# The first segment's P @ V runs: a fourth block only when more than ten blocks wait

## The chip, the cores and the metric

The kernel runs on one core of a Trainium2 chip. The metric is the device time of one launch in microseconds (us). Several launches are timed, and one more is taken with the hardware profiler; traces and profile pages come from that one.

## The reference

The input is one sequence of 2048 tokens with 512 features, all fp32. Two attention branches with 32 heads of 16 dimensions read the same `x`, and a gate per token mixes them:

```python
x = A_x
g = _sigmoid((x * gate_w).sum(-1, keepdims=True))
a = _A_ref(x, A_wqkv, A_wo)
b = _B_ref(x, B_wq, B_wk, B_wv, B_wo, B_beta)
return g * a + (1 - g) * b
```

`_A_ref` is plain softmax attention over all 2048 keys, with an output projection. `_B_ref` cuts the sequence into four segments of 512. In each it takes causal softmax attention within the segment, adds a read of a linear memory built from the earlier segments (`num / den`, mixed by `sigmoid(beta)`), and projects the result with its own `wo`.

## The kernel before

**Stages.** The first stage, up to about 345 us, computes Q, K and V of both branches (`pr`, line 312) and the memory terms, and writes them to DRAM. The second stage is the attention, and the change lies there. At the end come the output projections (`piece`, line 748), most of them laid between the attention's instructions.

**Units and slots.** The attention is cut into units. A unit is a side (A or B), a group of four heads (`g`, 8 of them) and a segment of 512 queries (`c`, 4 of them). A unit of A takes 64 slots, a unit of B takes 10. The order is A, B, A, B, and so on, so that a pair takes 74 slots; the first segment (`c` = 0) covers slots 0 to 591, since `first["A", 0, 1]`, the first slot of the second segment, is 8 x 74 = 592. In all there are 2368 slots.

**What a slot does.** The program is written out slot by slot, each engine in that order, by the loop at the end of `gated_mix`:

- `score_part(n)` puts one 128 x 512 tile of transposed scores into PSUM (matmul `st`, line 615, three buffers) and lets ScalarE take its exponential into `p` (line 638; 635 for some of B). Four slots fill one tile of `p`, of which there are six: four key-by-query blocks with four heads each. With a tile's last slot its four blocks go into `queue`, each with the slot from which it may be used (3 slots later for A, 5 for B). On side B, GpSimd first masks the diagonal (line 619).
- `max_part(n + 96)` runs 96 slots ahead. It puts scores in the other orientation into one of four PSUM banks (matmul `sm`, line 205), and VectorE reduces them to row maxima (line 220 for A; lines 235, 241 and 245 for B, where ScalarE and GpSimd prepare half of the tiles, lines 231 and 232). Every slot before the last 96 has one such tile.
- Once a unit's maxima are complete, they are merged (lines 181 to 189), transposed (`mt_ps`, line 195) and written into rows of `q`, so that the score matmul subtracts them itself.

The score matmuls contract over 48 or 50 rows at partitions 0 or 64; `st` and `sm` of one slot mostly lie in different halves of the array.

**Bursts and runs.** After every third slot comes a burst: `some_values` takes blocks from the head of `queue` and multiplies them with V (matmul `ops`, line 671, one PSUM bank). Blocks that are neighbours in one tile of `p` make one run of up to 512 columns, with one matmul for each of the four heads, at four column positions of the array; a run can't cross from one tile of `p` to the next. These are full fp32 matmuls, and the trace shows two records for each, so that one run of four heads reads "x8". A burst takes up to three blocks, and a fourth where more than six wait:

```python
some_values(n, MOST + (len(queue) > 6) if n < nS else 8)
```

A burst ends with the last block of a unit; ScalarE then copies the result out (line 675). The blocks that arrive (one per slot on average) and the three that a burst takes balance over three slots. `queue` counts all that wait, also those that may not be used yet. In the second and third segments other work takes the place of some bursts (`shared`), or is added to them (`fill`); in the first segment neither has an entry.

Of the kernel before, what the change touches and what calls it, by code (L numbers as in the profile page):

```python
# [37 lines left out]
MOST = 3  # L38
# [10 lines left out]
def gated_mix(ctx, tc, x, xT, wqkv, a_wo, b_wq, b_wk, b_wv, b_wo, beta, gate_w, out):  # L49
# [52 lines left out]
    first = {}  # L102
# [5 lines left out]
    nS = len(slots)  # L108
# [143 lines left out]
    def run_todo(m):  # L252

        for e in [e for e in todo if e[0] <= m]:
            todo.remove(e)
            e[1]()

    def run_late(pool, tag, m):
        for e in [e for e in late if e[0] < m]:
            late.remove(e)  # L260
            transpose_max(e[1], e[2], pool, tag)
# [3 lines left out]
    def loads(m):  # L265

        m = min(m, len(maxs) - 1)
        while loaded[0] <= m:
            u, (r, i) = maxs[loaded[0]]
            if loaded[0] == first_max[u]:  # L270
                load_q(u)
            kc = u[2] if u[0] == "B" else i // 8
            if (u, kc) not in kt_:
                load_k(u, kc)
            loaded[0] += 1
# [322 lines left out]
    queue = []  # L598
# [51 lines left out]
    def some_values(n, most):  # L650

        while queue and most and queue[0][0] <= n:
            _, u, i = queue.pop(0)
            most -= 1
            side, g, c = u
            w = 1
            while (queue and most and queue[0][0] <= n and queue[0][1] == u and (i + w) // 4 == i // 4
                   and (side == "A" or PIECES[i + w][0] == PIECES[i][0])):
                queue.pop(0)
                most -= 1  # L660
                w += 1
            p = pt_[u, i // 4]
            if side == "A":
                c0 = q0 = 128 * (i % 4)
                v = vt[u][:, i // 16, i // 4 % 4]
            else:
                b, c0, q0 = PIECES[i]
                v = vt[u][:, b]
            done = i + w == SLOTS[side]
            for h in range(4):  # L670
                nc.tensor.matmul(ops[32 * h:32 * h + 17, q0:q0 + 128 * w], v[:, 17 * h:17 * h + 17], p[:, h, c0:c0 + 128 * w],  # L671
                                 start=(i == 0), stop=done, tile_position=(0, 32 * h))
            if done:
                raw = ob.tile([128, CH], F32, tag="o", name="oraw")
                nc.scalar.copy(raw, ops)
                nc.sync.dma_start(od[side, c][4 * g:4 * g + 4].rearrange("h r t -> (h r) t"), raw)
                stored.add(u)
                if side == "B" and c and g % 2 == 0:
                    octet("M", g // 2, c, n + 4)
                if (side, g ^ 1, c) in stored and u != ("A", NG - 1, NCH - 1):  # L680
                    octet(side, g // 2, c, n + 8)
                if side == "A" and c - 1 in SHARED:
                    shared.extend(half_block(c - 1, g // 2, g % 2))
                return
# [89 lines left out]
    def half_block(c, b, half):  # L774

        ps = ops[:, 0:256]
        ks = [(side, o) for o in range(NO) for side in "AB"]
        for i in range(16):
            def f(i=i):
                piece(ps, *ks[i // 2], c, b, 2 * half + i % 2, i == 0, i == 15)  # L780
                if i == 15:
                    t = fr.tile([128, D], F32, tag="res", name="res", bufs=2)
                    nc.scalar.copy(t[:, 0:256], ps)
                    nc.sync.dma_start(out_rows(c, b)[:, 256 * half:256 * half + 256], t[:, 0:256])
            yield f
# [32 lines left out]
    def close(n, side, o, b, j):  # L818
        def f():
            if (side, o) == closing[0] and j == 0:  # L820
                assert len(free) == 4
            piece(banks[b], side, o, last, b, j, (side, o) == closing[0] and j == 0, (side, o) == closing[-1] and j == 3)
        fill.append((n, f))
    for side, o in closing[:-1]:
        for b in range(4):
            for j in range(4):
                close(max(tail0, end[side, 2 * o + 1, last] + 56), side, o, b, j)

    filled = [0]
    n = 0  # L830
    while n < nS or queue or beside or filled[0] < len(fill):
        for f in beside.pop(n, []):
            f()
        if n < nS:
            score_part(n)
        m = n + LEAD
        if m < nS:
            loads(m + PRE)

            def bank():  # L840
                i = free.pop(0)
                free.append(i)
                return banks[i]
            max_part(m, bank)
        run_todo(m)
        if n % BURST == BURST - 1 or n >= nS:
            if shared:
                for _ in range(4):
                    shared.pop(0)()
            else:  # L850
                some_values(n, MOST + (len(queue) > 6) if n < nS else 8)

            if any(e[0] < m + 1 for e in late):
                run_late(st_ps, "st", m + 1)
            else:
                for _ in range(1 if m < nS else 2):
                    if filled[0] < len(fill) and fill[filled[0]][0] <= n:
                        fill[filled[0]][1]()
                        filled[0] += 1
        n += 1  # L860
# [11 lines left out]
def build():  # L872
    import concourse.bacc as bacc
    nc = bacc.Bacc("TRN2", target_bir_lowering=False, num_devices=1)
    shapes = {"x": (S, D), "xT": (D, S), "wqkv": (D, 3 * D), "a_wo": (D, D), "b_wq": (D, D), "b_wk": (D, D),
              "b_wv": (D, D), "b_wo": (D, D), "beta": (H,), "gate_w": (D,)}
    args = [nc.dram_tensor(n, s, F32, kind="ExternalInput").ap() for n, s in shapes.items()]
    out = nc.dram_tensor("out", (S, D), F32, kind="ExternalOutput").ap()
    with tile.TileContext(nc) as tc:
        gated_mix(tc, *args, out)  # L880
    return nc
# [23 lines left out]
```

## Time and profile before

| | |
|---|---|
| three timed launches | 1939.02, 1941.87, 1943.77 us; median 1941.87 us |
| the profiled launch | 1940.47 us, its span 1938.8 us |
| mean granted TensorE clock | 0.993 |
| busy by engine | PE 98%, VectorE (DVE) 83%, ScalarE (ACT) 76%, GpSimd (POOL) 15% |

The span is the time from the program's first to its last instruction on the core; 1.67 us of the launch lie outside. The busy share of PE counts matmuls whose ends are modelled, and up to several of them overlap, so that it says less than that of VectorE and ScalarE. PEld is the weight load of a matmul, which may run beside an earlier matmul. In lists of instructions in order of time, neighbours of one kind are merged: "1.05 ... x8" is one run of eight records that took 1.05 us from the first start to the last (modelled) end.

### The profile page before, as it was taken

The numbers are of one execution on the slowest core, as the hardware profiler recorded it, in microseconds if no ns is written. First come the engines' busy times: TensorE is split into PE (matmuls) and PEld (weight loads), VectorE is DVE, ScalarE is ACT, GpSimd is POOL, SyncE is SP. The second block draws the span as 40 slices with busy tenths as digits, with TensorE's granted clock in tenths as the row PEclk, the third lists the DMA queues.
The fourth block names the chain that finished last, engine by engine and source line by source line (L and its number), as shares of the span: only waits on it lengthen the run. The fifth ranks groups of instructions, "written<-read, shape, count | busy, mean of one in ns | idle before, by whom it ended". The sixth has DMA issues, their size and how long they took to land.

```text
span 1938.8 us, 44063 instructions
## 1 busy us (share of the span) xinstructions
PE 1897.4 (98%) x17009; PEld 993.5 (51%) x17009; DVE 1611.9 (83%) x2768; ACT 1467.0 (76%) x2859; POOL 281.7 (15%) x497
## 2 busy tenths in 40 slices
PE   7999999999999999999999999999999999999997
PEld 6888766444444444444444444444444455555545
DVE  4235687899999999999999999999999889889810
ACT  3234432788888888888888888888888787878874
POOL 3000000211111111121111111111111111111210
PEclk9999999899999999999999999999999999999999
DMA  6667645434233334343444344434334333333211
GB/s 204 204 228 254 201 155 166 114 101 133 85 107 84 107 85 119 91 117 91 118 93 116 103 105 104 104 105 107 105 104 105 101 93 102 101 105 96 80 53 40
DMA packets 123632, 227.16 MB, mean 117 GB/s; under 512 B 35064, under 2 KB 48920, under 8 KB 122912
## 3 DMA queue, kind: packets, MB, share of 16 engines
q1 hardware_dynamic: 121840, 223.24, 41.0%
q8 instruction: 135, 2.21, 0.5%
q0 software_dynamic: 1296, 0.59, 0.2%
q14 instruction: 73, 0.60, 0.1%
q10 hardware_dynamic: 288, 0.52, 0.1%
HBM read 155.52 MB, written 67.52 MB: 115 GB/s over the span
## 4 chain that ended last, share of the span: by engine, by line
PE 89%; DMA 3%; ACT 3%; DVE 3%; issue 1%; POOL 0%; SPq 0%; ACTq 0%; POOLq 0%; DVEq 0%
PE ops L671 30%; PE st L615 27%; PE sm L205 14%; PE pr L312 11%; PE ops L748 3%; PE sm L748 2%; ACT p L638 2%; DVE pm L220 1%; DMA qdA<-q 1%; PE num L469 1%; DMA kdB<-q 1%; PE mt_ps L195 1%; ACT dg L231 1%; PE mps L500 0%; DMA qdB<-q 0%
## 5 line engine op out<-in xcount | busy, mean ns | idle before, releaser
L638 ACT ACTIVATE p<-st 128x512 f32<-128x512 f32 x2304 | 1219.5, 605 | 205.8 <-PE sm L205 168.7
L220 DVE TENSOR_REDUCE pm<-sm 128x1 f32<-128x512 f32 x2048 | 1286.5, 682 | 94.1 <-PE sm L205 71.3
L205 PE MATMUL sm<-kA,qA 48*128 48x512 f32 x2048 | 757.7, 450 | 1.3 <-DVE pm L220 1.3
L615 PE MATMUL st<-qA,kA 50*128 50x512 f32 x2048 | 702.9, 439 | 7.8 <-ACT p L638 7.1
L671 PE MATMUL ops<-p,vA 128*17 128x512 f32 (+2 forms) x4912 | 561.2, 529 | 0.0
L615 PEld LDWEIGHTS st<-qA,kA 50*128 50x128 f32 x2048 | 336.1, 186 | 412.6 <-ACT p L638 336.9
L205 PEld LDWEIGHTS sm<-kA,qA 48*128 48x128 f32 x2048 | 338.3, 185 | 37.7 <-DVE pm L220 22.9
L205 PE MATMUL sm<-kB,qB 48*128 48x128 f32 (+2 forms) x896 | 171.5, 295 | 0.6 <-DVE pmB L241 0.5
L671 PEld LDWEIGHTS ops<-p,vA 128*17 128x17 f32 x4912 | 81.7, 95 | 165.0 <-issue 153.9
L205 PEld LDWEIGHTS sm<-kB,qB 48*128 48x128 f32 x896 | 135.0, 188 | 10.6 <-DVE pm L220 2.6
L232 POOL TENSOR_SCALAR_AFFINE_SELECT dg<-dg 128x512 f32<-128x512 f32 x128 | 81.2, 637 | 301.2 <-ACT dg L231 299.6
L615 PE MATMUL st<-qB,kB 50*128 50x384 f32 (+3 forms) x512 | 120.9, 342 | 3.3 <-ACT p L638 2.4
L360 DVE TENSOR_TENSOR q<-pr,q 128x512 fp32r<-128x512 f32 x64 | 44.0, 687 | 90.8 <-ACT q L353 78.3
L353 ACT CAST q<-pr 128x512 fp32r<-128x512 f32 x64 | 37.5, 585 | 99.3 <-PE pr L312 63.6
L188 POOL CAST ms<-nm 128x16 fp32r<-128x16 f32 x64 | 12.6, 197 | 650.5 <-DVE nm L181 392.5
L615 PEld LDWEIGHTS st<-qB,kB 50*128 50x128 f32 x512 | 72.6, 186 | 66.3 <-ACT p L638 52.0
L619 POOL TENSOR_SCALAR_AFFINE_SELECT p<-p 128x512 f32<-128x512 f32 x128 | 78.7, 634 | 95.6 <-ACT p L638 95.0
L671 PE MATMUL ops<-p,vB 128*17 128x512 f32 (+3 forms) x1024 | 89.2, 444 | 1.7 <-issue 1.5
L241 DVE TENSOR_REDUCE pmB<-sm 128x4 f32<-128x512 f32 x128 | 87.1, 681 | 1.2 <-PE sm L205 1.2
L235 DVE TENSOR_REDUCE pmB<-dg 128x4 f32<-128x512 f32 x128 | 86.7, 677 | 0.8 <-POOL dg L232 0.8
L231 ACT COPY dg<-sm 128x512 f32<-128x512 f32 x128 | 76.4, 597 | 1.8 <-DVE pmB L235 1.8
L722 DVE RECIPROCAL rec<-rec 128x32 f32<-128x32 f32 x44 | 15.1, 343 | 71.2 <-DMA rec<-odA 40.3
(129 smaller groups left out, 1567.5 us busy)
## 6 DMA issues: line engine op xcount, KB each, us to landing
kA<-kdA SPq DMA_DIRECT2D x256, 128.0 KB
vA<-vdA SPq DMA_DIRECT2D x32, 544.0 KB
kA<-kdA SPq DMA_DIRECT2D x256, 64.0 KB
qdA<-q SPq DMA_DIRECT2D x32, 256.0 KB
kdA<-q SPq DMA_DIRECT2D x32, 256.0 KB
qdB<-q SPq DMA_DIRECT2D x32, 256.0 KB
qA<-qdA SPq DMA_DIRECT2D x64, 128.0 KB
kdB<-q SPq DMA_DIRECT2D x32, 256.0 KB
```

The costliest lines, as they stand in the source:

```text
L205: nc.tensor.matmul(ps[:, n0:n0 + n], rows(qt[u][:, :, s * 128:(s + 1) * 128], h, 48), rows(k[:, :, k0:k0 + n], h, 48), start=True, stop=True)
L220: nc.vector.tensor_reduce(pm[:, h, s, kc:kc + 1], ps, axis=AX.X, op=ALU.max)
L231: nc.scalar.copy(dg, blocked(ps))
L232: nc.gpsimd.affine_select(out=dg, in_=dg, pattern=[[0, 4], [-1, 128]], base=0, channel_multiplier=1, compare_op=ALU.is_ge, fill=MASKED)
L235: todo.append((m + MASK_T, lambda: nc.vector.tensor_reduce(to, dg.rearrange("p (h s) t -> p h s t", h=2), axis=AX.X, op=ALU.max)))
L241: nc.vector.tensor_reduce(pm[:, 1, h, 3:7], blocked(ps), axis=AX.X, op=ALU.max)
L312: nc.tensor.matmul(ps, l(a, k), r(b, k), start=(n == 0), stop=(n == 11))
L615: nc.tensor.matmul(ps[:, n0:n0 + CH - q0], rows(k[:, :, b * 128:(b + 1) * 128], h, 50), rows(q[:, :, q0:], h, 50), start=True, stop=True)
L619: nc.gpsimd.affine_select(out=x, in_=x, pattern=[[0, 4], [1, 128]], base=0, channel_multiplier=-1, compare_op=ALU.is_ge, fill=0.0)
L638: nc.scalar.activation(p[:, h], ps, AF.Exp, scale=SCALE)
L671: nc.tensor.matmul(ops[32 * h:32 * h + 17, q0:q0 + 128 * w], v[:, 17 * h:17 * h + 17], p[:, h, c0:c0 + 128 * w], start=(i == 0), stop=done ...
L748: nc.tensor.matmul(ps[32 * t:32 * t + 32, 128 * (j % (ps.shape[1] // 128)):128 * (j % (ps.shape[1] // 128)) + 128], held[side, c][:, o, 12 ...
```

## The change

A function gives the limit above which a burst takes a fourth block: ten for slots of the first segment, six as before for all later ones.

```diff
+    def jam(n):
+
+        return 10 if n < first["A", 0, 1] else 6
+
...
-                some_values(n, MOST + (len(queue) > 6) if n < nS else 8)
+                some_values(n, MOST + (len(queue) > jam(n)) if n < nS else 8)
```

## The prediction

> **What bounds the kernel now.** I first read the page's busy shares, then the busy time of each engine in stretches of the first segment (which the trace shows from 345 to about 730 us), then what VectorE waits for there, and last the instructions in order of time around single bursts.
>
> ```profile
> span 1938.8 us, 44063 instructions
> PE 1897.4 (98%) x17009; PEld 993.5 (51%) x17009; DVE 1611.9 (83%) x2768; ACT 1467.0 (76%) x2859; POOL 281.7 (15%) x497
> ```
>
> PE looks full, but its ends are modelled. The stretches say more (busy us of each engine; I cut them where one pair of units passes into the next, and between):
>
> ```profile
> core 0: us, PE busy (x) PEld busy (x) DVE busy (x) ACT busy (x) POOL busy (x), PEclk, DMA share, GB/s
> 425.00:445.00 20.00, 18.83 (x157) 8.84 (x155) 18.52 (x32) 18.33 (x38) 5.40 (x10) 1.00 0.11 36
> 446.00:470.00 24.00, 24.00 (x193) 10.18 (x187) 23.93 (x44) 19.70 (x39) 1.28 (x1) 1.00 0.65 174
> 472.00:493.00 21.00, 20.25 (x167) 9.52 (x164) 19.34 (x33) 19.32 (x40) 6.57 (x11) 1.00 0.34 90
> 494.00:516.00 22.00, 22.00 (x190) 8.80 (x189) 22.00 (x38) 19.18 (x39) 0.00 (x0) 1.00 0.48 135
> ```
>
> Between the passages (446 to 470, 494 to 516) VectorE is never idle: 23.93 of 24.00 and 22.00 of 22.00 us. There the row maxima set the pace, and nothing on PE can make it faster. In the passages VectorE is idle for 1.5 us of 20 and 1.7 of 21. So the change can gain only there and at the start. How much there is to gain, 365 to 730 us, by groups and by VectorE's waits (the list of waits leaves out the short ones):
>
> ```profile
> L220 DVE TENSOR_REDUCE pm<-sm 128x1 f32<-128x512 f32 x495 | 308.1, 681 | 12.9 <-PE sm L205 9.8 <-PE st L615 1.1
> L671 PE MATMUL ops<-p,vA 128*17 128x512 f32 x692 | 91.2, 598 | 0.0
> L671 PE MATMUL ops<-p,vA 128*17 128x384 f32 x296 | 31.1, 492 | 0.0
> L671 PE MATMUL ops<-p,vA 128*17 128x128 f32 x296 | 15.3, 278 | 0.0
> ```
> ```profile
> DVE pm L220 <- PE sm L205: 9.8, 23, 1.1
> DVE pm L220 <- PE st L615: 1.1, 5, 0.3
> ```
>
> At most 12.9 us of VectorE's idle time stand before its main reduction, nearly all of it ended by a matmul: PE was late. The 28 listed stalls hold 10.9 us. The three rows of line 671 show the pattern of today's bursts: at eight records a run, 86 runs of four blocks, 37 of three and 37 of one.
>
> **What a burst costs PE.** Here are bursts of one, four and three blocks one after another, and one of B with 4 followed by one of B with 3 and 1:
>
> ```profile
> 423.44 3.07 DVE L220 TENSOR_REDUCE pm<-sm 128x1 f32<-128x512 f32 x5
> ...
> 423.95 0.41 PE L671 MATMUL ops<-p,vA 128*17 128x128 f32 x8
> ...
> 424.29 0.49 PE L615 MATMUL st<-qA,kA 50*128 50x512 f32 x1
> ...
> 425.98 1.05 PE L671 MATMUL ops<-p,vA 128*17 128x512 f32 x8
> 426.43 0.21 DVE L183 TENSOR_REDUCE nm<-pmB 128x16 f32<-128x64 f32 x1
> ...
> 426.96 0.49 PE L615 MATMUL st<-qA,kA 50*128 50x512 f32 x1
> ...
> 427.53 3.85 DVE L220 TENSOR_REDUCE pm<-sm 128x1 f32<-128x512 f32 x6 [0.29 <-PE sm L205]
> ...
> 427.86 1.05 PE L671 MATMUL ops<-p,vA 128*17 128x512 f32 x8
> ...
> 429.75 0.84 PE L671 MATMUL ops<-p,vA 128*17 128x384 f32 x8
> ...
> 430.52 0.18 PEld L615 LDWEIGHTS st<-qA,kA 50*128 50x128 f32 x1 [0.64 <-ACT p L638]
> ...
> 431.54 0.69 DVE L220 TENSOR_REDUCE pm<-sm 128x1 f32<-128x512 f32 x1 [0.16 <-PE st L615]
> ```
> ```profile
> 396.50 1.05 PE L671 MATMUL ops<-p,vB 128*17 128x512 f32 x8
> 397.48 0.49 PE L615 MATMUL st<-qA,kA 50*128 50x512 f32 x1
> ...
> 398.43 1.06 PE L671 MATMUL ops<-p,vB 128*17 128x384 f32 x16
> 399.42 0.50 PE L615 MATMUL st<-qA,kA 50*128 50x512 f32 x1
> ```
>
> From a run's start to the next score: one block 0.34 us (423.95 to 424.29), three 0.77 (429.75 to 430.52), four 0.98 (425.98 to 426.96). So a block is worth 0.21 us, and 0.13 us is the burst's own. The second fence prices a split: 3 and 1 in two runs take 0.99 us, 4 in one run 0.98; by the rounding a split costs 0 to 0.02 us, and I take 0.015.
>
> VectorE needs 2.99 us for five tiles (423.44 to 426.43), 0.598 each, thus 1.79 us for the three slots of a burst. Two bursts of four stand 1.88 us apart (425.98 to 427.86): PE then falls 0.09 us behind VectorE each time, and VectorE waits (0.29 us at 427.53). With three blocks the distance would be 1.88 - 0.98 + 0.785, about 1.68 us, less than 1.79. The burst of one, 423.95, is followed by the next only 2.03 us later; of these 1.69 lie behind its run, where the burst of four needs 0.90, so PE idles there for some 0.79 us.
>
> **The change, part by part.** I followed the rule of the queue slot by slot. Up to slot 591 the four-block bursts of A (4, 4, 3, 1 in turn) become 3, 1+2, 2+1, 3, since the limit of ten is almost never passed. The blocks stay the same 592; the runs grow from 195 to 293, the bursts that do anything from 188 to 195 of 197, the splits within bursts from 7 to 98. Later slots change in one run.
>
> - *Work added to PE:* 91 splits x 0.015 = 1.4 us; 7 to 8 bursts more at 0.13 us, 1.0, up to 1.9 with the drain ahead of a run. Together 2.3 to 3.3 us. Between passages, where VectorE sets the pace, it is free: two splits in four bursts are 0.03 us, against 0.79 us of idling once in these four. Were that cover gone, the whole 3.3 us would count.
> - *Work evened out:* a four-block burst of A loses one block, 0.98 to 0.785, so 0.2 us; the one-block burst grows by 0.43, which its 0.79 us of idling takes in. A stall of VectorE behind a four-block burst can shrink by 0.2 us. In order of time about three of four stalls stand behind such a burst: 21 of the 28 x 0.2 = 4.2 us. Of the 2.0 us too short to be listed (12.9 - 10.9) half, 1.0.
> - *The start:* TensorE's clock is half here (the column PEclk, 0.50), so that the first four-block run takes 1.91 us, and VectorE waits longest. One block less is 0.4 us at that clock, and the next burst gives 0.2: 0.6 us. Bounds 0 and 2.2, the stall itself.
>
> ```profile
> 347.00:353.00 6.00, 5.61 (x26) 3.27 (x26) 2.97 (x5) 5.71 (x12) 2.45 (x5) 0.50 0.89 235
> ...
> 351.37 1.91 PE L671 MATMUL ops<-p,vA 128*17 128x512 f32 x8
> ...
> 353.86 1.29 DVE L220 TENSOR_REDUCE pm<-sm 128x1 f32<-128x512 f32 x2 [2.23 <-PE st L615]
> ```
>
> - *The passage into B:* where B's first four blocks come early, PE waits for GpSimd's mask, and the burst after it is empty. With the change the queue still holds a block of A there: a run of one stands in the first burst, three blocks of B in the second. PE's wait of 0.51 us goes, three times in eight (the pattern repeats every third pair), and with it the stall of 0.30 behind it: 0.9 us. What is late next is PE's own work in the burst that was empty.
>
> ```profile
> 442.06 1.05 PE L671 MATMUL ops<-p,vB 128*17 128x512 f32 x8 [0.51 <-issue]
> ...
> 443.68 1.89 DVE L220 TENSOR_REDUCE pm<-sm 128x1 f32<-128x512 f32 x3 [0.30 <-PE sm L205]
> ...
> 445.65 1.06 PE L671 MATMUL ops<-p,vB 128*17 128x384 f32 x16
> ```
>
> - *Nothing else:* at most 12 blocks wait, four tiles of `p` with the one being filled, and there are six, so ScalarE waits for no tile. Loads, their queues and the copies out keep their order; a copy out (line 675) comes one burst later. Blocks are older when used, so no run waits longer for its exponentials.
>
> Sum: 4.2 + 1.0 + 0.6 + 0.9 less 0.7 for splits and refilled bursts inside the passages = 6.0 us gained. Against the profiled launch of 1940.47 us that is 1934.5; against the median of 1941.87 us, 1.4 us higher, it is 1935.9, which I give. All later segments only start earlier.
>
> **The rivals.** *(1) PE never falls behind.* Lateness adds up over bursts; if every burst is below 1.79 us, the passages may be taken almost whole. The cap is 12.9 us, plus up to 2.2 at the start; two thirds give -10 us, 1932. Against it: passages hold other PE work (transposes, B's small matmuls), and VectorE waits behind a three-block burst too (0.16 us after the one at 429.75). *(2) The stalls only move.* If PE is full for the whole passage, its total work counts, not its order; over a passage that work falls only by what the queue holds back, one to three blocks, 0.2 to 0.6 us, in some of eight passages, and 1 or 2 us come back with the splits: 1940 to 1942. Speaking for it: the stretch of 425 to 445 has a stall behind almost each burst. *(3) Slower: the empty bursts are missed.* At each passage one burst is empty today (between 442.06 and 445.65 none stands in 3.59 us), and there PE catches up. The change fills these eight with one to four blocks, 0.34 to 0.98 us each, 5.5 to 6.5 us in all. It decides where PE comes to that burst late by more than the 0.9 us it holds; then 6 us and the 1.4 of splits are paid against the 2 us won elsewhere: +5 us, up to +8, 1947 to 1950. Against it: VectorE is full right after the passage, so PE is ahead by then. *(4) A split costs as much as a burst.* At 0.13 us for each of 98 runs, 12.7 us would be on PE, 1949 if half of it is on the path. The pair 0.99 against 0.98 us speaks against it.
>
> [...]
>
> **How the numbers follow.** A difference of 0.3% (5.8 us) is about what a measurement of this kernel can tell from no change. The forecast has 0.50, with a range of its own from -11 to -1 us (1931 to 1941); its middle lies just beyond 5.8, so 0.30 of it counts as faster and 0.20 as the same. Rival 1 has 0.17 (faster), rival 2 0.18 (same), rival 3 0.11 and rival 4 0.04 (both slower). Together 0.47, 0.38, 0.15. The range takes in rival 1 down to -14 us and rival 2, and leaves out most of rivals 3 and 4: 1928 to 1945.
>
> **What would show it.** Right: in the first segment line 671 has runs of 128, 256 and 384 columns and nearly none of 512; the idle time before line 220 from 365 to 730 us falls from 12.9 to about 7 us; a burst of 1+2 takes about 0.785 us to the next score; the wait of 0.51 us before B's first run is gone; and from 730 us on all is the same, some 6 us earlier. Wrong: stretches like 446 to 470 show VectorE idle (PE has become the bound), or new stalls stand behind the formerly empty bursts, or a split costs more than 0.03 us.

## The result and the profile after

| | before | changed |
|---|---|---|
| timed launches, median | 1940.3 us (1937.71 to 1945.12, 22) | 1937.53 us (1932.58 to 1941.58, 22) |
| ratio, 95% interval | | 0.998 [0.9972, 0.9988] |
| profiled launch, span | 1938.8 us | 1934.8 us |
| granted clock, profiled launch | 0.993 | 0.993 |

The ratio, one of means, is a gain of 3.9 us (2.3 to 5.4); the medians lie 2.8 us apart. By the bound of 0.3% this counts as the same, to which the prediction gave 0.38 against 0.47 for faster, and it is clear of zero. The forecast was 6.0 us, 1935.9 us in all; that 1937.53 us lies so near to it is partly luck, since the median of before came out 1.6 us lower over 22 launches than over the first three.

The first segment of the changed kernel, 365 to 730 us: groups of instructions (busy us, mean ns, idle time before them), then VectorE's waits (us in all, times, longest).

```profile
L220 DVE TENSOR_REDUCE pm<-sm 128x1 f32<-128x512 f32 x498 | 309.8, 680 | 10.0 <-PE sm L205 4.7 <-PE st L615 3.4
L671 PE MATMUL ops<-p,vA 128*17 128x384 f32 x672 | 71.2, 496 | 0.0
L671 PE MATMUL ops<-p,vA 128*17 128x256 f32 x624 | 48.4, 382 | 0.0
L671 PE MATMUL ops<-p,vA 128*17 128x128 f32 x672 | 34.4, 277 | 0.0
L671 PE MATMUL ops<-p,vA 128*17 128x512 f32 x16 | 2.1, 598 | 0.0
```
```profile
DVE pm L220 <- PE sm L205: 4.7, 11, 0.8
DVE pm L220 <- PE st L615: 3.4, 9, 0.6
```

The pattern is as forecast: two runs of 512 columns are left of 86. VectorE's idle time before its main reduction fell from 12.9 to 10.0 us, its listed stalls from 28 with 10.9 us to 20 with 8.1. Each of the two sums holds about 1.1 us that belongs to a half-clock phase (before: one stall at 539.99 us; changed: 0.61 and 0.51 us at 366.83 and 369.22 us, in or just behind the phase at the start), so that 2.9 us is also the fall without them. So the mechanism is there, with half the forecast size.

Two passages and the stretches behind them, some 2 us later than in the prediction's fence, since the changed kernel's profile is behind there (below; columns as in that fence):

```profile
427.00:447.00 20.00, 19.97 (x202) 10.21 (x194) 18.92 (x33) 18.77 (x40) 5.42 (x11) 1.00 0.08 25
448.00:472.00 24.00, 24.00 (x249) 12.21 (x247) 23.93 (x44) 20.14 (x40) 1.28 (x1) 1.00 0.56 160
474.00:495.00 21.00, 20.92 (x213) 10.71 (x215) 19.91 (x34) 19.10 (x41) 6.99 (x13) 1.00 0.35 89
496.00:518.00 22.00, 22.00 (x233) 11.03 (x229) 22.00 (x37) 19.66 (x38) 0.00 (x0) 1.00 0.45 135
```

Between the passages VectorE is busy for 23.93 of 24.00 us and 22.00 of 22.00, exactly as before: the added splits are hidden there. In the passages it went from 18.52 to 18.92 of 20, and from 19.34 to 19.91 of 21.

The bursts themselves (PE in order of time):

```profile
405.39 0.84 PE L671 MATMUL ops<-p,vA 128*17 128x384 f32 x8
406.16 0.50 PE L615 MATMUL st<-qA,kA 50*128 50x512 f32 x1
...
407.15 0.84 PE L671 MATMUL ops<-p,vA 128*17 128x128 f32 x16
407.92 0.50 PE L615 MATMUL st<-qA,kA 50*128 50x512 f32 x1
```

Three blocks in one run and 1+2 in two runs both take 0.77 us to the next score. A split costs no more than the rounding, 0.01 us.

**Where the profiled span went.** I took the start of the exponential of a slot as a clock hand for both traces. The changed kernel's slot 0 comes 0.6 us later (347.33 against 346.74), slot 45 already 3.3 us later (381.39 against 378.11), slot 622 is 0.4 us earlier (746.50 against 746.93), slot 2250 1.1 us earlier, and the last slot 2.8 us earlier (1911.13 against 1913.91). So the first 45 slots lost 2.7 us, the passages won 3.7, and slots 2250 to the last won another 1.7 in work that the change doesn't touch; the rest of the 4.0 us lies in smaller pieces (0.7 us from slot 622 to 2250, 1.2 behind the last slot, 0.6 lost ahead of slot 0). The losses and gains at start and end go with the clock: the next stretch is the start of both, before first; PEclk is the last column but two.

```profile
345.00:373.00 28.00, 25.96 (x177) 12.27 (x176) 23.05 (x40) 22.09 (x43) 8.25 (x14) 0.82 0.56 141
```
```profile
345.00:373.00 28.00, 26.35 (x185) 14.65 (x189) 20.47 (x36) 19.50 (x37) 8.25 (x14) 0.63 0.44 123
```

TensorE ran at half clock there for 10.2 us before, in two phases of 6.8 and 3.4 us (a mean of 0.82 over 28 us), and for 20.5 us in one after (0.63). At the end before has a half-clock phase at 1862 us (PEclk 0.72 from 1861 to 1867 us), just where it falls back by 1.6 us (slots 2250 to 2324), and the changed kernel has none there (1.00 from 1860 to 1870 us). Of the 3.7 us won in the passages, about 1.1 are a half-clock phase of before at 537.6 us (0.57 from 537 to 541 us); 2.6 are left.

### The profile page after: what moved, and what is told of

The parts are those of the page before. It is cut to its first block, busy times and chain, and to the rows that moved or that the text cites. A ratio compares the mean times of both kernels' runs of the same rounds, so it can differ in the third digit from the quotient of the medians.

```text
span 1934.8 us, 45638 instructions
## 1 busy us (share of the span) xinstructions
PE 1900.4 (98%) x17801; PEld 1022.0 (53%) x17801; DVE 1611.7 (83%) x2768; ACT 1468.8 (76%) x2859; POOL 281.9 (15%) x497
## 4 chain that ended last, share of the span: by engine, by line
PE 91%; DMA 2%; DVE 2%; ACT 2%; issue 1%; SPq 0%; POOL 0%; ACTq 0%; DVEq 0%; POOLq 0%
PE ops L671 30%; PE st L615 27%; PE sm L205 15%; PE pr L312 12%; PE ops L748 3%; PE sm L748 2%; ACT p L638 1%; DVE pm L220 1%; DMA qdA<-q 1%; PE num L469 1%; PE mps L500 1%; PE mt_ps L195 1%; ACT dg L231 0%; DMA qdB<-q 0%; DMA kdA<-q 0%
## 5 line engine op out<-in xcount | busy, mean ns | idle before, releaser
L671 PE MATMUL ops<-p,vA 128*17 128x512 f32 (+3 forms) x5616 | 564.4, 485 | 0.0
L671 PEld LDWEIGHTS ops<-p,vA 128*17 128x17 f32 x5616 | 101.3, 96 | 172.5 <-issue 152.9
L671 PE MATMUL ops<-p,vB 128*17 128x128 f32 (+3 forms) x1112 | 88.0, 415 | 0.3
```

## The experiments

Each execution comes with its span and granted clock, so that the time at half clock can be worked out: (1 - clock) x 1935 us x 2, 1935 us standing for any of the spans. The factor 2 comes from the traces of before and changed, in which the clock is recorded as 0.50 or 1.00 and nothing else. Over all launches of all kernels here the time follows it with 0.27 us for each us at half clock (correlation 0.80, means of each kernel removed). The last column takes that out: the difference of means to before at equal half-clock time, with twice its standard error. It is worked out afterwards, against all 85 launches of before whose clock is on record; the ratio beside it is the measurement, against the 22 to 32 launches of before that were timed with the kernel. The kernels below have 5 (hold2, mask7_hold2) to 12 launches each, the changed one 22. "Idle" is the idle time before line 220 from 365 to 730 us in the profile (12.9 before, 10.0 changed).

| kernel | median us | ratio to before [95%] | half-clock us, mean | idle us | at equal half clock |
|---|---|---|---|---|---|
| before (85 launches) | 1941.24 | | 29.6 | 12.9 | |
| changed | 1937.53 | 0.998 [0.9972, 0.9988] | 32.0 | 10.0 | -5.0 +- 0.6 |
| passages | 1938.96 | 0.9989 [0.9981, 0.9998] | 33.1 | 9.2 | -3.1 +- 1.3 |
| between | 1945.58 | 1.0021 [1.001, 1.0032] | 40.6 | 12.3 | +0.9 +- 0.8 |
| between2 | 1946.08 | 1.0016 [1.0005, 1.0027] | 41.0 | 15.3 | +1.0 +- 0.8 |
| split | 1941.01 | 0.9997 [0.9988, 1.0005] | 26.4 | 12.0 | -0.2 +- 0.9 |
| hold2 | 1934.29 | 0.9965 [0.9953, 0.9976] | 27.9 | 5.9 | -7.2 +- 1.5 |
| hold4 | 1942.94 | 1.0003 [0.9992, 1.0015] | 30.0 | 11.5 | +1.2 +- 0.8 |
| dglast | 1937.42 | 0.9976 [0.9963, 0.9989] | 29.0 | 7.8 | -4.0 +- 0.8 |
| hold2_dglast | 1936.76 | 0.9971 [0.9957, 0.9984] | 30.1 | 9.5 | -5.0 +- 0.8 |
| start_only | 1946.57 | 1.0028 [1.0017, 1.0039] | 44.8 | 15.8 | +1.4 +- 0.8 |
| start_apart | 1937.5 | 0.9982 [0.9973, 0.999] | 31.0 | 8.7 | -4.1 +- 1.0 |
| mask7 | 1936.64 | 0.9974 [0.9965, 0.9983] | 32.0 | 11.5 | -5.6 +- 0.6 |
| mask7_hold2 | 1925.6 | 0.9918 [0.9905, 0.9932] | 21.7 | 3.3 | -13.6 +- 0.8 |

The expectations below count 2.0 to 2.3 us of idle time per passage for before. The 12.9 us of the table over eight passages are 1.6 each, so the two aren't the same count; changes against before can be compared.

**Where in the segment: passages, between.** The theory of the prediction was that the passages from one pair of units to the next pay. The rival was that the start, or chance in the clock, does.

```diff
-        return 10 if n < first["A", 0, 1] else 6
+        inside = n % 74 >= 45 or (n >= 74 and n % 74 < 6)
+        return 10 if n < first["A", 0, 1] and inside else 6      # passages
+        return 10 if n < first["A", 0, 1] and not inside else 6  # between
```

> Limit ten only around the passages from one pair of units to the next (the last 29 slots of a pair and the first 6 of the following), first segment; six elsewhere, so that the start and the stretches between passages are as before. If the gain of the change is made in the passages, whether by shorter bursts or by blocks held back: VectorE's idle time per passage falls from 2.0-2.3 to about 1.7 us as in the changed kernel, and the time is 2.5 to 4 us below before, with 41 more runs in place of 98. If the gain came from the start or from the length of the half-clock phase there: no difference to before, within 1.5 us.

> The complement: limit ten in the first segment outside the passages only (start and stretches between), six in the passages. VectorE sets the pace there, so both theories of the passages expect nothing: within 1.5 us of before, idle time per passage 2.0 to 2.3 us as before (up to 0.5 more in every third passage, which takes 31 blocks in place of 28). If levelling between passages is what pays: 2.5 to 4 us faster.

Passages brought 2.1 us (0.4 to 3.7), a little short of what was expected, and the stalls fell to 9.2 us. Between brought none of the gain: its stalls stayed at 12.3 us. It was 4 us slower, which neither theory had.

> The kernel of between once more, for a second profile. It was 4 us slower in the timed launches, while its profile showed the first segment no longer than before. If the 4 us come from TensorE's half-clock phases, they show here as phases within 365 to 730 us, each a step of 1 to 1.5 us in the time of a slot against before. If they are a lasting cost of the bursts: the same ratio, and steps at the passages without such phases. If the first measurement was off: a ratio within 0.1% of 1.

The second time was as slow (1.0016), so the first was no mistake. Its half-clock time didn't lie where I expected it, in phases between 365 and 730 us, but at the start: one phase of 27.3 us from 345.9 us on, PEclk 0.52:

```profile
345.00:373.00 28.00, 26.79 (x170) 14.95 (x171) 18.65 (x32) 18.33 (x36) 8.26 (x14) 0.52 0.44 112
```

The launches agree: 40.6 and 41.0 us at half clock against 29.6. At 0.27 us each that is 3 of the 4 us.

**The start: start_only, start_apart.** Both kernels that begin with bursts of three had long half-clock phases in their profiles (20.5 us in the changed one, 13.7 and 27.3 us in the two of between). Is that their price?

```diff
-        return 10 if n < first["A", 0, 1] else 6
+        return 10 if n < 45 else 6                          # start_only
+        return 10 if 45 <= n < first["A", 0, 1] else 6      # start_apart
```

> Limit ten in the first 45 slots only (six elsewhere): the start of the changed kernel, with the rest of before. In the profiles so far, TensorE's half-clock phase at the start lasted 20.5, 13.7 and 27.3 us in the three kernels that start with bursts of three (the changed one and between, twice), 10.2 to 13.7 us in the kernels that start with bursts of four. If bursts of three at the start prolong that phase: 17 to 27 us of it here, and a time 2 to 4 us above before. If those lengths were chance: 10 to 14 us, and within 1 us of before.

> Limit ten from slot 45 to 591, six in the first 45 slots: the changed kernel with the start of before. If bursts of three cost half-clock time at the start: a half-clock phase of 10 to 14 us, slot 45 within 1 us of before, and 5 to 7 us below before, better than the changed kernel. If the start makes no difference: the changed kernel's 2.5 to 5 us below before. Idle time per passage as in the changed kernel, 1.7 to 1.8 us.

start_only is slower, 1.0028 [1.0017, 1.0039], 5.4 us where 2 to 4 were expected, with 27.3 us at half clock at the start of its profile and 44.8 us in all per launch: bursts of three at the start alone do harm. In all fourteen profiles, phases longer than 13.7 us at the start stand only in those that begin with bursts of three (20.5, 27.3 and 27.3 us; the fourth, between, had 13.7). start_apart has the short phase (13.7 us, slot 45 within 1.3 us of before), but is no faster than the changed kernel: 0.9982 against 0.998. In 22 launches the changed kernel spends only 32.0 us at half clock, although its first 45 slots are those of start_only. Why the same start goes with 11 to 15 us more of half clock than before in between and start_only, where the passages are as before, and with 2 in the changed kernel, stays open.

The burst itself does gain at the start, at equal clock. Where the clock was half all through the first burst, VectorE's stall behind it is 2.49 to 2.52 us in the nine profiles with four blocks there, and 2.06 to 2.10 in the four with three (start_apart, then changed):

```profile
354.12 1.29 DVE L220 TENSOR_REDUCE pm<-sm 128x1 f32<-128x512 f32 x2 [2.52 <-PE sm L205]
```
```profile
354.31 1.29 DVE L220 TENSOR_REDUCE pm<-sm 128x1 f32<-128x512 f32 x2 [2.10 <-PE sm L205]
```

That of before, 2.23 us, is shorter than the others because its clock rose at 353.3 us, ahead of the stall's end. And with a phase of 13.7 us each, slots 0 to 45 took 31.4 us in between, with bursts of three, and 32.5 to 32.7 us in the seven kernels with bursts of four. Part of that is the clock as well: 11.6 us of the phase lay behind slot 0 in between, 12.0 to 12.9 in the others. So something below 1 us is won there at equal clock, by one profile with bursts of three, and in the other three a longer half-clock phase takes it back.

**Is it the split? split.** Bursts as before, runs of two blocks at most:

```diff
-            while (queue and most and queue[0][0] <= n and queue[0][1] == u and (i + w) // 4 == i // 4
+            while (queue and most and queue[0][0] <= n and queue[0][1] == u and (i + w) // 4 == i // 4
+                   and (n >= first["A", 0, 1] or w < 2)
```

> Bursts as before, but in the first segment no run is longer than two blocks: 338 runs in place of 195, 143 more splits than before and nothing else. At 0.015 us each that is 2.1 us of PE work, of which less than half lies in passages: 0 to 1 us slower than before, and a burst of 2+2 takes 1.00 us to the next score in place of 0.98. If a split costs as much as a burst of its own (0.13 us): 18.6 us of PE work, 8 us slower or more.

143 splits cost nothing that can be measured (0.9997 [0.9988, 1.0005], so at most 1.0 us, 0.007 us each), and a burst of 2+2 takes 0.99 us to the next score, against 0.98:

```profile
426.55 1.06 PE L672 MATMUL ops<-p,vA 128*17 128x256 f32 x16
427.54 0.50 PE L615 MATMUL st<-qA,kA 50*128 50x512 f32 x1
```

That settles rival 4, which had 0.13 us for each run.

**Long bursts or much work? hold2, hold4.** Is it the single long burst that makes VectorE wait, or all the work that PE has in a passage? hold2 takes two blocks a burst in the passages, hold4 four and none in turn, each with one more where more than 13 wait. The diff has the line of each.

```diff
+    def most(n):
+        q = n % 74
+        if n < first["A", 0, 1] and (q >= 52 or (n >= 74 and q < 3)):
+            return 2 + (len(queue) > 13)                             # hold2
+            return 4 * (n // 3 % 2 == 0) + (len(queue) > 13)         # hold4
+        return MOST + (len(queue) > 6)
...
-                some_values(n, MOST + (len(queue) > 6) if n < nS else 8)
+                some_values(n, most(n) if n < nS else 8)
```

> Before's rule, but from slot 52 of a pair to slot 2 of the next bursts of the first segment take two blocks (three where more than 13 wait), and the queue is worked off after the passage in bursts of four. The passage has 22 to 24 blocks of P @ V in place of 28 (28 to 30 in the changed kernel). If PE's whole work in the passage sets the stalls there: 0.9 us less work per passage, idle time per passage 0.8 to 1.2 us, time 8 to 10 us below before. If only the longest bursts count: the stalls that single three- and four-block bursts cause go, idle time per passage about 1.5 us, 4 to 5 us below before. If neither (passage set by ScalarE or GpSimd): no gain over the changed kernel, 2.5 to 4 us below before.

> As hold2, but the bursts in a passage take four blocks and none in turn (one more where more than 13 wait), so that about as few blocks (21 to 24) fall into the passage as with hold2, in long bursts. If the length of single bursts makes the stalls: idle time per passage stays at 1.8 to 2.2 us, the time within 2 us of before. If the work that PE has over the whole passage makes them: idle time per passage 1.2 to 1.6 us as with hold2 or less, the time 5 to 8 us below before.

hold2 gains 6.8 us (4.7 to 9.1), more than the changed kernel, and its stalls fall to 5.9 us. hold4 gains nothing (1.0003), although as few blocks lie in its passages (by the rule of the queue, slot 52 of a pair to slot 2 of the next: 16 to 20 in hold4 and hold2, 20 to 27 before): 11.5 us of stalls are back, 9.7 of them behind bursts of four or five blocks. The two groups, hold2 first:

```profile
L220 DVE TENSOR_REDUCE pm<-sm 128x1 f32<-128x512 f32 x505 | 314.6, 682 | 5.9 <-PE sm L205 4.1 <-PE st L615 0.6
```
```profile
L220 DVE TENSOR_REDUCE pm<-sm 128x1 f32<-128x512 f32 x495 | 308.9, 680 | 11.5 <-PE sm L205 8.7 <-PE st L615 1.4
```

So it is the length of single bursts in the passages, not the number of blocks there; an empty burst before a long one does not make up for it. hold2 alone would not have told the two apart: its 6.8 us lie between what the two theories gave. Two blocks are not short enough everywhere: 3.8 of the 5.9 us left stand behind bursts of two.

**What makes a passage? dglast, hold2_dglast, mask7, mask7_hold2.** All twelve stalls of more than 0.25 us that hold2 left, slot by slot, stand before the maximum tile one slot behind slot 48, 55, 62 or 69 of a pair. Those are the slots of B's masked maximum tiles: ScalarE copies such a tile (line 231), GpSimd masks it (232), and VectorE reduces it only eight slots later (235), so that the slot itself gives VectorE nothing.

```diff
-        theirs = {r: [(unit("B", b), (r, i)) for b in bs for i in range(5)] for r in range(2)}
+        theirs = {r: [(unit("B", b), (r, i)) for b in bs for i in ((2, 3, 4, 0, 1) if 2 <= k <= 9 else range(5))] for r in range(2)}
```

> Bursts as before. In the first segment's passages only the order of B's maximum tiles is turned: the four tiles that ScalarE copies and GpSimd masks before VectorE may reduce them (lines 231, 232, 235) come last of the ten, so that they fall into slots 16 to 37 of the next pair, between the passages; the work is the same. If what remains of VectorE's stalls comes from these four tiles, each of which gives VectorE nothing to do for eight slots: idle time per passage falls from 2.0-2.3 to below 1.2 us, time 5 to 8 us below before. If the transposes and B's scores make the passage: idle time as before, and the time within 1.5 us of before.

The stalls move with the four tiles. In the stretch from 425 to 445, where before VectorE was busy for 18.52 of 20 us, it is now busy for 19.95, and the next stretch, full before, has them (dglast; windows, then VectorE in order of time):

```profile
425.00:445.00 20.00, 19.75 (x153) 8.67 (x153) 19.95 (x35) 17.37 (x36) 2.92 (x6) 1.00 0.12 36
446.00:470.00 24.00, 23.79 (x203) 10.06 (x194) 23.32 (x42) 21.86 (x44) 3.80 (x5) 1.00 0.68 181
```
```profile
454.33 3.84 DVE L220 TENSOR_REDUCE pm<-sm 128x1 f32<-128x512 f32 x6 [0.38 <-PE sm L205]
458.34 0.69 DVE L220 TENSOR_REDUCE pm<-sm 128x1 f32<-128x512 f32 x1 [0.17 <-PE st L615]
458.95 0.68 DVE L235 TENSOR_REDUCE pmB<-dg 128x4 f32<-128x512 f32 x1
```

The transposes and B's scores, still in their old place, cost next to nothing by themselves: in the old passages VectorE is idle for 0.0 to 0.1 us each (before 1.3 to 1.7, half-clock stall left out). The whole gained 4.7 us (2.1 to 7.2), perhaps since the four tiles now stand apart from the transposes; no run shows that. Together with hold2, which shortens bursts where the tiles no longer are, it gains no more:

> hold2 and dglast together. If both are right and independent (blocks held back and four tiles moved out): idle time per passage below 0.6 us, 10 to 14 us below before. If they take the same stalls away: no more than the better of the two, 6 to 8 us below before.

0.9971 is between the two alone (0.9965 and 0.9976). In the old passages no idle time is left for hold2 to take, and the blocks that it holds back are worked off in bursts of four where the tiles now are: idle time there rises from 7.8 to 9.5 us. The last idea was to let the masked reduction of one tile fall into the empty slot of the next, in all segments:

```diff
-MASK_T = 8
+MASK_T = 7
```

> Bursts as before in the whole kernel. Only the delay after which VectorE reduces a masked tile is changed, in all segments: seven slots in place of eight (MASK_T). These tiles stand seven slots apart, so that the reduction of one then comes just in the slot of the next, which gives VectorE nothing to do. If the holes that the four tiles leave are the stalls: three of four are filled, idle time per pair falls from 2.0-2.3 to 0.6-1.2 us, 8 to 11 us less in the first segment, and 10 to 30 us in all, by how far VectorE sets the pace later. If the stalls come from ScalarE's extra copy or from PE's order: no change in the first segment, within 1.5 us of before in all.

> mask7 with the held-back blocks of hold2 in the first segment: the two best edits together. If the two add up: idle time per pair below 0.7 us in the first segment, 2 to 5 us faster than mask7. If mask7 leaves hold2 nothing to take: the same as mask7 within 1.5 us.

mask7 gains 5.0 us (3.3 to 6.8), but not where I expected: in the first segment the stalls only fell to 11.5 us, and its profile gains steadily in the later segments (some 5 us from slot 770 to slot 2250, against before). So filling the holes is not enough with bursts of four. With hold2 it nearly is: 3.3 us of stalls are left,

```profile
L220 DVE TENSOR_REDUCE pm<-sm 128x1 f32<-128x512 f32 x507 | 314.8, 684 | 3.3 <-PE sm L205 0.9 <-PE st L615 0.7
```

and 0.9918 [0.9905, 0.9932], 16 us, is the best version here, 11 us better than mask7 where 2 to 5 were expected. The same place in hold2, then with mask7: the masked reduction (line 235) now comes ahead of the tile that VectorE had waited for.

```profile
478.75 0.69 DVE L220 TENSOR_REDUCE pm<-sm 128x1 f32<-128x512 f32 x1 [0.73 <-PE sm L205]
479.35 0.68 DVE L235 TENSOR_REDUCE pmB<-dg 128x4 f32<-128x512 f32 x1
```
```profile
479.05 0.68 DVE L235 TENSOR_REDUCE pmB<-dg 128x4 f32<-128x512 f32 x1
479.86 3.88 DVE L220 TENSOR_REDUCE pm<-sm 128x1 f32<-128x512 f32 x6
```

Of hold2's twelve stalls above 0.25 us, the eight behind slots 55, 62 and 69, the slots that mask7 fills, are down to at most 0.13; the four behind slot 48, which it doesn't fill and whose burst still has four blocks, stay at 0.28 to 0.33. ScalarE's copies of the masked tiles are the same in both, so that with short bursts they don't make these eight. How much they add with bursts of four wasn't tested.

At equal half clock the two edits add up: 7.2 + 5.6 against 13.6 us. The rest of the 16 is less time at half clock, 21.7 us against 29.6.

## Why the prediction came out as it did

- **VectorE sets the pace between passages, splits are hidden there: right.** 23.93 of 24.00 us busy before and after; split measured zero.
- **The pattern and the price of a burst: right.** 0.77 us for 1+2 where 0.785 was forecast, 0.01 us or less a split where 0.015 was taken.
- **Four-block bursts make VectorE late (4.2 + 1.0 us): right in kind, too large.** hold4 brings the stalls back with the bursts. But the sum let each stall shrink by 0.2 us on its own. The listed stalls fell by 2.8 us, all idle time of that group by 2.9. These 2.9 hold the passage into B too; with that term (0.9) and the 0.7 us taken off, 5.4 us were forecast for the passages. Part of what is missing is rival 2, stalls that move on: in the changed kernel a stall of 0.59 us stands behind the burst that grew from one block to three.

```profile
440.04 3.25 DVE L220 TENSOR_REDUCE pm<-sm 128x1 f32<-128x512 f32 x5
443.88 0.69 DVE L220 TENSOR_REDUCE pm<-sm 128x1 f32<-128x512 f32 x1 [0.59 <-PE sm L205]
```

- **The passage into B (0.9 us): the wait went, the gain didn't.** The idle time before B's first runs, 1.5 us in all, is 0.1 now (the row of before, then of the changed kernel). The trace of before doesn't show it as a wait for GpSimd's mask: that mask (line 619) ran from 440.08 to 440.71 us, and what ended just ahead of the run at 442.06 us was ScalarE's copy out of `ops` (line 675, 441.33 to 441.96 us). But the stalls of 0.14 and 0.30 us at 440.91 and 443.68 us before became the 0.59 above, a burst earlier: 0.15 us lost, not won.

```profile
L671 PE MATMUL ops<-p,vB 128*17 128x512 f32 x64 | 9.2, 646 | 1.5 <-issue 1.5
```
```profile
L671 PE MATMUL ops<-p,vB 128*17 128x384 f32 x104 | 10.9, 489 | 0.1
```

- **What a passage is: wrong.** Transposes and B's small matmuls were named as what keeps PE late; dglast shows that the stalls go where the four masked tiles go, and hold4 and mask7_hold2 that long bursts and the slots without work for VectorE make them together.
- **The start (+0.6 us): right at equal clock, but the time at half clock was taken as given.** The 0.4 us of the first burst are there (2.52 against 2.10), and the profiled start still lost 2.7 us, to twice the time at half clock (20.5 against 10.2 us). The 22 launches show only 2.4 us more half clock than before, 0.65 us, so what the start was worth in them stays open.
- **Rival 3, the formerly empty bursts: not seen.** The stretches behind the passages are as full as before (VectorE 23.93 of 24.00 and 22.00 of 22.00 us).

So 6.0 against 3.9 us is a sum of a true mechanism, whose passage terms came to 2.9 us in place of 5.4; that the total is not further off is in part luck, for the launches gained about 1 us more than these stalls. The last column of the table would put it at 5.0 us at equal half clock (some 0.5 less against the 22 launches of before timed with it, if those had as much half clock as the 85); the stalls account for about 3 of those, and what the rest is the runs don't show.

## What to carry to other kernels

Where two engines are nearly even, ask which instruction leaves the pacing engine without work, and look at where its stalls stand, slot by slot, before putting them down to what else happens there. A stall that stands behind a long burst isn't always won back by the amount by which the burst is shortened: the next burst can inherit the lateness, as here, where stalls of 0.14 and 0.30 us became one of 0.59. Changes of some 0.2%, 3.9 us here, are of the size of a few half-clock phases (0.9 us for one of 3.4 us, at 0.27), so work out each launch's time at reduced clock before reading a difference.

## What the hardware showed that I had not expected

The half-clock phases: those seen are multiples of 3.4 us long. The traces have phases of 3.4 and 6.8 us in before and of 3.4 and 20.5 us in the changed kernel; 13.7 and 27.3 us were seen in others. A launch has 22 to 45 us of them on the mean of a kernel. The times of launches of one kernel, which spread over 4 to 9 us (11.5 us in the 85 of before), go with them at 0.27 us for each us; with a correlation of 0.80 that is about two thirds of their variance.

I found nothing that sets their length. From 345 to 373 us, PE was shown busy for 26.79 of 28 us in between2, with 27.3 us at half clock (PEclk 0.52); in before for 25.96 us, with 10.2 (0.82); in hold2 for 27.64 us, with 13.7 (0.76):

```profile
345.00:373.00 28.00, 27.64 (x172) 14.00 (x172) 21.96 (x38) 21.78 (x41) 8.25 (x14) 0.76 0.53 133
```

Three of the four profiles that begin with bursts of three have a longer phase there than any that begins with bursts of four. So the time at half clock doesn't follow the busy time that the profile shows for PE; what it does follow these runs don't show.
